# Banded attention with a gated feed-forward block: probabilities turned over by VectorE in 32x32 blocks, values laid per block of 32 keys, and the weighting done in tiles of 32x64 of the array in one visit per group

## The chip, the cores and the metric

The kernel runs on one core of one Trainium2 chip. The metric is the device time of one execution in microseconds (us); a lower time is better. The core has five engines that run at once and wait for each other through semaphores: TensorE (PE in the profile, with its weight loads shown apart as PEld), VectorE (DVE), ScalarE (ACT), GpSimd (POOL) and SyncE (SP), whose queue issues most of the DMAs here.

## The reference: what is computed

Eight batches, eight heads, 576 positions, 64 numbers per head, all float32.

```
scores = q @ k^T / 8                                  # per batch and head, 576 x 576
heads 0-3: keys 0..31 back;   heads 4-7: keys 0, 4, 8, ... 124 back (32 keys each)
attn = softmax(masked scores);   x = attn @ v         # joined over heads: 576 x 512 per batch
h = relu(x @ w_in)            # 512 -> 1024, halves u and v
v_n = (v - mean) / sqrt(var + 1e-6)                   # over the 512 features
v_s = w_spatial @ v_n + b_spatial                     # mixes the 576 positions
out = (u * v_s) @ w_out                               # 512 -> 512
```

So each query looks at 32 keys, its own band. With the positions of heads 4-7 sorted by their residue modulo 4, that band is a plain band too: a block of 32 queries needs the 64 keys of its own block and of the block before.

## The kernel before, in words

**Data.** `NB` = 18 blocks of 32 queries per head. Heads go in pairs (`NPAIR` = 4 per batch): 64 numbers of one head on partitions 0-63, the other's on 64-127. Two pairs make a group (`NG` = 2 per batch), so there are 16 groups in all.

**Scores, `unit` (L417).** A group has `NU` = 3 units; each covers 6 of the 18 blocks, for both pairs and both heads of a pair, by 24 float32 matmuls (L437) with 64 rows and 32 columns of the array. In a score tile the partitions are four sets of 32 queries, and along a row lie `US` = 3 tiles by 2 heads by `KW` = 64 keys: 384 numbers. For the first two batches (`early`) a bfloat16 matmul against the mask stands ahead of each score matmul (L436), and ScalarE takes the exponential straight from PSUM; later batches add the mask on VectorE (L474). Then come the row maximum, the exponential, the row sum, its reciprocal (L484) and the product on GpSimd (L486): the probabilities `p`.

**Turning over.** The weighting needs keys on the partitions. Three TensorE transposes per unit (L491, 128x128, against `ident`) put `p` into a PSUM bank, and ScalarE copies the bank to `pT` (L494): keys of head j on partitions 64j to 64j+63.

**Values, `values_in` (L405).** Each pair has its own buffer: for each block of queries the 64 keys that it needs, head 0 on partitions 0-63 and head 1 on 64-127. Blocks overlap by 32 keys, so each value is loaded twice. Four DMAs per pair, in pieces of 64 numbers.

**Weighting, `weighted` (L500).** Two visits per group, one for each half of the blocks (`HB` = 9). A visit has 36 float32 matmuls (L517), each over 64 keys and giving 64 x 32 numbers, on four tiles of 64 rows by 64 columns of the array. A float32 matmul shows in the trace as two weight loads (PEld) and two multiplications (PE), so a visit is `x72` there. `evacuated` (L533) then splits the result into two parts, `xth` on ScalarE (L543) and `xtl` on VectorE (L256), for the feed-forward block; every large matmul of that block is done in three passes over such parts.

**The rest.** `v_tile` makes the v half (L569, L583), `gate` the u half (L637) and the spatial mix (L648 to L650) with their product (L653), `project` the output (L673, L677, and the store L679). `weight` splits the weights at the start, on ScalarE (L295, L334) and VectorE (L297 to L328) or GpSimd (L312 to L318). `warm` (L689) multiplies zeros at the start.

**What sets the order.** Every piece of work is a generator (a strand) that yields the engine and a cost that it expects, or the buffers that it needs. `Timeline.run` plays these costs through and issues whatever could start first, with a bonus for a lower rank. So the order on each engine is fixed at build time by a table of costs: transposes of a unit 0.45 us on PE and 0.48 us on ACT, a weighting visit 0.9 us. Buffers that are in short supply: 8 PSUM banks, six `kqv` buffers shared by queries with keys and by values, three `p` and four `pT`. At the start the list `first` (L698 to L713) sets the order of the loads.

Of the kernel before, what the change touches and what calls it, by code (L numbers as in the profile page):

```python
# [12 lines left out]
F32 = mybir.dt.float32  # L13
# [108 lines left out]
def tile_banded_attention_gated_moe(  # L122
# [33 lines left out]
    NB = S // QB  # L156
    NS = NB // 2
    US = 3
    NU = NS // US
    NG = NPAIR // 2  # L160
    NC = DM // P
# [5 lines left out]
    EPS = 1e-6  # L167

    BIG = NB * D

    const = ctx.enter_context(tc.tile_pool(name="const", bufs=1))
    work = ctx.enter_context(tc.tile_pool(name="work", bufs=2))
# [2 lines left out]
    def bufs(tag, shape, n, pool=const):  # L175
        return [pool.tile(shape, F32, name=f"{tag}{i}") for i in range(n)]
# [6 lines left out]
            bank=bufs("bank", [P, 512], 8, ps),  # L183
            mm=[None] * 4,
            s=[None] * 2,
            pt=[None] * 2,
            av=[None] * 4,
            wk=[None] * 1,
            kqv=bufs("kqv", [P, WIN + 2 * S], 6),
            stage=[t[:, n * BIG : (n + 1) * BIG] for t in stage for n in range(2)],  # L190
            mid=bufs("mid", [P, 512], 6),
            p=bufs("p", [P, US, 2, KW], 3),
            pT=bufs("pT", [P, US, P], 4),
            ur=bufs("ur", [P, HS], 4),
            ob=bufs("ob", [P, HS], 2),
        )
# [30 lines left out]
            g, row = divmod(c, QB)  # L227
            cut.update({(far, g): 2, (far, g + 1): 3} if row else {(far, g): 1})
    for (far, g), n in cut.items():
        r = slice(g % 2 * 2 * QB, g % 2 * 2 * QB + 2 * QB)  # L230
        nc.vector.tensor_copy(masks[r, US * far + g // 2], kinds[r, n])
    ident = const.tile([P, P], F32, name="ident")
    make_identity(nc, ident)
    same = const.tile([P, P], BF16, name="same")
    nc.vector.tensor_copy(same, ident)
    halfneg = const.tile([P, 1], F32, name="halfneg")
    nc.gpsimd.memset(halfneg, -0.5)

# [143 lines left out]

    used, keys, values = {}, {}, {}

    def heads_in(b, hp, lo=0, hi=NU):

        if lo == 0:
            yield "kqv"
        else:
            yield [("qk", b, hp, lo - 1)]  # L390
        got = yield DMA, 0.83 * (hi - lo), 1.5
        if lo == 0:
            used[b, hp] = got
            keys[b, hp] = got[0][1]
        kq = keys[b, hp]
        w = S // NU
        kc = slice(lo * w + WIN * (lo > 0), hi * w + WIN)
        nc.sync.dma_start(kq[:, kc], kT[b, hp, :, kc])
        nc.sync.dma_start(
            kq[:, WIN + S + lo * w : WIN + S + hi * w].rearrange("p (u c) -> p u c", c=w), qT[b, hp, :, lo:hi]  # L400
        )
        for u in range(lo, hi):
            tl.done("qk", b, hp, u)

    def values_in(b, hp):  # L405

        yield "kqv"
        (big,) = yield DMA, 2.5, 1.5
        src = vw[b, hp].rearrange("k (t j d) -> k t j d", j=2, d=D)
        dst = big[1][:, :BIG].rearrange("p (t n d) -> p t n d", n=2, d=D)  # L410
        for j in range(2):
            for n in range(2):
                nc.sync.dma_start(dst[j * D : j * D + D, :, n, :], src[n * QB : n * QB + KW, :, j, :])
        values[b, hp] = big
        tl.done("values", b, hp)

    def unit(b, G, u):  # L417

        n = (b, G, u)
        pairs = (2 * G, 2 * G + 1)  # L420
        yield [("qk", b, hp, u) for hp in pairs] + ([("v", 0, 1)] if b == 1 else [])
        yield "s bank bank p"
        early = b < 2
        *held, pb = yield PE, 1.1 if early else 0.9
        s = [h[:, : US * KW].rearrange("p (e k) -> p e k", e=US) for _, h in held[1:]]
        for e in range(US):
            for q in range(4):
                g = 2 * (US * u + e) + q // 2
                kq = keys[b, pairs[q % 2]]
                for j in range(2):  # L430
                    r = slice(j * D, j * D + D)
                    if early:

                        kind = cut.get((G >= NG // 2, g), 0)
                        one = same[r, j * D : j * D + QB]
                        nc.tensor.matmul(s[j][q * QB : q * QB + QB, e, :], one, kinds[r, kind], start=True, stop=False)  # L436
                    nc.tensor.matmul(  # L437
                        s[j][q * QB : q * QB + QB, e, :],
                        kq[r, WIN + S :].rearrange("p (u n i t) -> p u t n i", n=2, i=QB, t=US)[:, u, g // 2 % US, g % 2],
                        kq[r, g * QB : g * QB + KW],  # L440
                        start=not early,
                        stop=True,
                    )
# [40 lines left out]
        nc.vector.reciprocal(rv, sm)  # L484
        yield POOL, 0.88
        nc.gpsimd.tensor_mul(flat, flat, rv.unsqueeze(2).broadcast_to([P, 2 * US, KW]))  # L486
        yield "pt bank pT"
        *held, probs[n] = yield PE, 0.45
        pp = held[1][1][:, : US * P].rearrange("k (e q) -> k e q", e=US)
        for e in range(US):  # L490
            nc.tensor.transpose(pp[:, e, :], p[:, e].rearrange("p j k -> p (j k)"), ident)  # L491
        tl.give(pb)
        yield ACT, 0.48
        nc.scalar.copy(probs[n][1], pp)  # L494
        tl.give(*held)
        tl.done("pT", *n)

    probs = {}

    def weighted(b, G, rank):  # L500

        pairs = (2 * G, 2 * G + 1)
        for h in range(2):
            blocks = range(h * HB, h * HB + HB)
            units = sorted({g // 2 // US for g in blocks})
            yield [("pT", b, G, u) for u in units] + [("values", b, hp) for hp in pairs]
            yield "av bank av bank"
            got = yield PE, 0.9
            acc = [got[:2], got[2:]]
            for g in blocks:  # L510
                u, e = divmod(g // 2, US)
                for i, hp in enumerate(pairs):
                    v = values[b, hp][1][:, :BIG].rearrange("p (g d) -> p g d", g=NB)
                    q = g % 2 * 2 + i
                    for j in range(2):
                        r = slice(j * D, j * D + D)
                        nc.tensor.matmul(  # L517
                            acc[j][1][1][i * D : i * D + D, (g - h * HB) * QB : (g - h * HB + 1) * QB],
                            v[r, g, :],
                            probs[b, G, u][1][r, e, q * QB : q * QB + QB],  # L520
                            start=True,
                            stop=True,
                        )
            for u in range(NU):
                if u * US * 2 + US * 2 - 1 in blocks:
                    tl.give(probs[b, G, u])
            if h:
                for hp in pairs:
                    tl.give(values[b, hp])
            for j in range(2):  # L530
                tl.add(rank, evacuated(b, 2 * G + j, h, acc[j]))

    def evacuated(b, hp, h, acc):  # L533
        xh, xl = xt[b % 2]
# [160 lines left out]
    AO, AS = 0.1, 0.6  # L695
    tl.add(0.5, warm())

    first = [heads_in(0, hp, lo, hi) for lo, hi in ((0, 1), (1, NU)) for hp in (0, 1)]  # L698
    halves = {}
    for half in (1, 0):  # L700
        cols = slice(half * NF, half * NF + NF)
        for c in range(NC):

            heads = [c // 2 * 4 + c % 2 + n for n in (0, 2)]
            src = tuple(w_in[h * D : h * D + D, half] for h in heads)
            halves[half, c] = weight_in(("wi", half, c), src)
# [13 lines left out]
    for b in range(B):  # L720
        for hp in range(NPAIR):
            r = b - 1 + AO + AS * hp / NPAIR
            if b:
                tl.add(r, heads_in(b, hp))
                tl.add(r, values_in(b, hp))
# [78 lines left out]
```

## Time and profile before

| | |
|---|---|
| runs of the kernel before | 587.33, 583.3, 587.29 us; median 587.29 |
| the profiled execution | 584.25 us, of which the span from first to last instruction is 582.4 us |
| granted TensorE clock, mean over the span | 0.976 |
| busy in the span: PE, PEld, DVE, ACT, POOL | 547.7, 506.8, 324.1, 242.6, 139.1 us |
| one batch in the steady part (for instance from 394.7 to 459.3 us) | 64.6 us |

How to read it: each engine works through its own instructions in order, so an engine that is late holds up all that is queued behind it. The share of busy time is a mean over stages that have different limits. Here there are two: a start of about 104 us, in which weights are loaded and split while the first batches go through attention, and a long part in which one batch's feed-forward block runs beside the attention of batches ahead. Rows of the timeline give start, duration, engine, line and operation; the durations of TensorE instructions overlap, so a stretch of TensorE work is read from one start to the next.

### The profile page before, as it was taken

The page shows a single profiled execution, that of the slowest core. Times are in us where ns is not written, and L with a number is a line of the kernel's source. Part 1 is how long each engine was busy: PE and PEld are TensorE (multiplying, and loading weights), DVE is VectorE, ACT ScalarE, POOL GpSimd, SP SyncE. Part 2 cuts the span into 40 slices and gives each one's busy share as a digit, 9 for nine tenths or more (in the row PEclk, how much of TensorE's full clock was granted, in tenths as well). Part 3 has the DMA queues.
Part 4 walks back from the last instruction along what each step waited for, and adds up shares of the span by engine and source line. Part 5 has one row for each costly group of instructions (what it writes and reads, how often), then busy time and mean ns, then how long its engine had stood idle before and what let it go on. Part 6 is the DMA issues. An engine that isn't in the chain of part 4 may idle for free.

```text
span 582.4 us, 18304 instructions
## 1 busy us (share of the span) xinstructions
PE 547.7 (94%) x7971; PEld 506.8 (87%) x7971; DVE 324.1 (56%) x775; ACT 242.6 (42%) x620; POOL 139.1 (24%) x163
## 2 busy tenths in 40 slices
PE   9786537999999999999999999999999999999997
PEld 7565537998999989999999989999999989999997
DVE  3799977334863366434863376444863466444411
ACT  3764856433444334333434344343443334423321
POOL 2112987001421023201420033201420132201000
PEclk9979688999999999999999999999999999999999
DMA  8986481631345203731345104731365003101011
GB/s 238 217 218 174 138 215 42 161 93 42 85 119 150 55 12 98 194 83 42 85 130 149 44 12 107 185 84 42 84 156 137 31 19 78 43 1 42 1 42 41
DMA packets 97444, 56.66 MB, mean 97 GB/s; under 512 B 78290, under 2 KB 87506, under 8 KB 97364
## 3 DMA queue, kind: packets, MB, share of 16 engines
q1 hardware_dynamic: 88148, 46.06, 32.2%
q10 hardware_dynamic: 9216, 9.44, 4.6%
q8 instruction: 62, 1.02, 0.7%
q14 instruction: 18, 0.15, 0.1%
HBM read 46.04 MB, written 9.44 MB: 95 GB/s over the span
## 4 chain that ended last, share of the span: by engine, by line
PE 85%; DVE 8%; ACT 2%; DMA 1%; POOL 1%; issue 1%; SPq 1%; ACTq 0%; DVEq 0%; POOLq 0%
PE bank L637 17%; PE bank L648 17%; PE bank L673 17%; PE bank L569 13%; PE bank L517 6%; PE bank L437 5%; PE bank L491 3%; PE bank L689 2%; PE bank L583 2%; PE bank L650 1%; PE bank L649 1%; DVE mid L297 1%; DMA out_dram<-ob 1%; DMA stage<-in_b_sp_dram 1%; DVE bank L299 1%
## 5 line engine op out<-in xcount | busy, mean ns | idle before, releaser
L604 POOL TENSOR_TENSOR rs<-rs,halfneg 128x1 f32<-128x1 f32 (+1 forms) x40 | 31.2, 782 | 245.5 <-DVE rs L602 245.5
L637 PE MATMUL bank<-xth,wih 128*128 128x288 f32 x256 | 79.5, 310 | 0.0
L648 PE MATMUL bank<-wth,vnh 128*128 128x288 f32 x256 | 79.5, 310 | 0.0
L653 DVE TENSOR_TENSOR ur<-ur,bank 128x288 f32<-128x288 f32 x64 | 28.7, 449 | 87.5 <-PE bank L650 87.4
L648 PE MATMUL bank<-wtl,vnh 128*128 128x288 f32 x256 | 76.5, 299 | 0.0
L648 PE MATMUL bank<-wth,vnl 128*128 128x288 f32 x256 | 76.4, 299 | 0.0
L637 PE MATMUL bank<-xth,wil 128*128 128x288 f32 x256 | 75.9, 297 | 0.4 <-issue 0.4
L673 PE MATMUL bank<-gh,woh 128*128 128x288 f32 x256 | 76.2, 298 | 0.0
L637 PE MATMUL bank<-xtl,wih 128*128 128x288 f32 x256 | 76.0, 297 | 0.0
L673 PE MATMUL bank<-gl,woh 128*128 128x288 f32 x256 | 75.7, 296 | 0.1
L673 PE MATMUL bank<-gh,wol 128*128 128x288 f32 x256 | 75.6, 295 | 0.0
L486 POOL TENSOR_TENSOR p<-p,rv 128x384 f32<-128x384 f32 x48 | 40.3, 841 | 80.8 <-DVE rv L484 74.1
L659 ACT CAST gh<-ur 128x288 fp32r<-128x288 f32 x64 | 27.6, 433 | 64.2 <-DVE ur L653 64.2
L569 PE MATMUL bank<-wih,xth 128*128 128x512 f32 x128 | 50.7, 396 | 0.9 <-DVE xtl L256 0.9
L569 PE MATMUL bank<-wil,xth 128*128 128x512 f32 x128 | 50.2, 392 | 0.0
L637 PEld LDWEIGHTS bank<-xth,wih 128*128 128x128 f32 x256 | 48.6, 190 | 1.8 <-ACT p L461 0.2
L569 PE MATMUL bank<-wih,xtl 128*128 128x512 f32 x128 | 50.2, 392 | 0.0
L648 PEld LDWEIGHTS bank<-wth,vnh 128*128 128x128 f32 x256 | 49.0, 191 | 0.8 <-issue 0.2
L437 PEld LDWEIGHTS bank<-kqv 64*32 64x32 f32 x2304 | 32.1, 124 | 20.0 <-issue 19.6
L517 PEld LDWEIGHTS bank<-pT,kqv 64*64 64x64 f32 x2304 | 38.5, 139 | 12.5 <-issue 4.8
L677 ACT COPY ob<-bank 128x288 f32<-128x288 f32 x64 | 25.5, 399 | 57.1 <-PE bank L673 40.5
L648 PEld LDWEIGHTS bank<-wtl,vnh 128*128 128x128 f32 x256 | 49.1, 192 | 0.2
(101 smaller groups left out, 1215.9 us busy)
## 6 DMA issues: line engine op xcount, KB each, us to landing
kqv<-in_vw_dram SPq DMA_DIRECT2D x128, 144.0 KB, 4.1
out_dram<-ob ACTq DMA_DIRECT2D x64, 144.0 KB, 1.7
kqv<-in_kT_dram SPq DMA_DIRECT2D x30, 304.0 KB, 3.3
kqv<-in_qT_dram SPq DMA_DIRECT2D x30, 288.0 KB, 4.3
stage<-in_w_in_dram SPq DMA_DIRECT2D x16, 256.0 KB, 5.3
stage<-in_w_out_dram SPq DMA_DIRECT2D x4, 512.0 KB, 3.5
stage<-in_w_spT_dram SPq DMA_DIRECT2D x5, 288.0 KB, 3.3
kqv<-in_kT_dram SPq DMA_DIRECT2D x2, 192.0 KB, 3.5
```

Source lines behind the costliest of these rows:

```text
L437: nc.tensor.matmul(s[j][q * QB : q * QB + QB, e, :], kq[r, WIN + S :].rearrange("p (u n i t) -> p u t n i", n=2, i=QB, t=US)[:, u, g // 2 ...
L486: nc.gpsimd.tensor_mul(flat, flat, rv.unsqueeze(2).broadcast_to([P, 2 * US, KW]))
L491: nc.tensor.transpose(pp[:, e, :], p[:, e].rearrange("p j k -> p (j k)"), ident)
L517: nc.tensor.matmul(acc[j][1][1][i * D : i * D + D, (g - h * HB) * QB : (g - h * HB + 1) * QB], v[r, g, :], probs[b, G, u][1][r, e, q * QB ...
L569: nc.tensor.matmul(pm, x[a][:, c, cols], wi[w][:, c, NF:], start=c == 0 and n == 0, stop=c == NC - 1 and n == 2)
L604: nc.gpsimd.tensor_tensor(rs[:m], rs[:m], halfneg[:m], op=ALU.pow)
L637: nc.tensor.matmul(pu, wi[w][:, c, fs], x[a][:, c, ts], start=n == 0, stop=n == 3 * NC - 1)
L648: nc.tensor.matmul(pv, vn[c][a][:, fs], wt[w][:, c, ts], start=n == 0, stop=False)
L653: nc.vector.tensor_mul(ur, ur, pv)
L659: nc.scalar.copy(gated[0][:, f, ts], ur)
L673: nc.tensor.matmul(po, wo[w][:, f, ds], gated[a][:, f, ts], start=n == 0, stop=n == 3 * NC - 1)
L677: nc.scalar.copy(ob[1], po)
```

## The change

The probabilities are no longer transposed as a whole. VectorE turns each 32x32 block over where it stands (one instruction of 128x384 per unit, `STREAM_TRANSPOSE`, from one `p` buffer into a second one). Within a set of 32 partitions, keys then lie on the partitions and queries along the row, in four pieces: two heads by two blocks of 32 keys. The transposes on TensorE, their PSUM bank, the copy on ScalarE and `pT` go; there are seven `p` buffers.

So that each of the four sets of 32 partitions has its own values, these are laid per block of 32 keys: set `h * 2 + i` holds half `h` of the blocks of pair `i`, ten blocks with both heads side by side (640 numbers). Each value is loaded once but for the block at the seam. One buffer per group, four DMAs of 32 partitions each, in pieces of 128 numbers. The units' blocks are dealt accordingly: partitions 0-63 take blocks of the first half, 64-127 of the second.

The weighting is one visit per group. Each of the nine tiles has two key blocks by two heads by four sets: 144 float32 matmuls per group with 32 rows and 64 columns of the array and 32 numbers along the row, where there were 72 with 64 rows. The two key blocks are added up in PSUM. Eight tiles of the array are in use instead of four, and four PSUM banks are held at a time, as many as two visits held.

Queries and keys of a pair are loaded by two DMAs from the start, where the first two pairs had them in two parts, and the list `first` is in another order. A part of `w_in` is loaded by one DMA of 128 rows, not by two of 64, since the order of the heads in `x` is now the plain one.

```diff
-            pt=[None] * 2,
-            kqv=bufs("kqv", [P, WIN + 2 * S], 6),
+            kq=bufs("kq", [P, WIN + 2 * S], 4),
+            v=bufs("v", [P, NK, 2 * D], 2),
-            p=bufs("p", [P, US, 2, KW], 3),
-            pT=bufs("pT", [P, US, P], 4),
+            p=bufs("p", [P, US, 2, KW], 7),
...
+    def values_in(b, G):
+        yield "v"
+        (values[b, G],) = yield DMA, 2.6, 1.5
+        v = values[b, G][1]
+        for h in range(2):
+            for i in range(2):
+                src = vw[b, 2 * G + i].rearrange("(r k) (t c) -> k r t c", r=3, c=2 * D)
+                dst = v[(h * 2 + i) * QB : (h * 2 + i + 1) * QB].rearrange("k (r t) c -> k r t c", r=2)
+                nc.sync.dma_start(dst, src[:, h : h + 2, h * (HB // 2) : h * (HB // 2) + NK // 2])
...
-                g = 2 * (US * u + e) + q // 2
+                g = US * u + e + q // 2 * HB
...
         nc.gpsimd.tensor_mul(flat, flat, rv.unsqueeze(2).broadcast_to([P, 2 * US, KW]))
-        yield "pt bank pT"
-        *held, probs[n] = yield PE, 0.45
-        pp = held[1][1][:, : US * P].rearrange("k (e q) -> k e q", e=US)
-        for e in range(US):
-            nc.tensor.transpose(pp[:, e, :], p[:, e].rearrange("p j k -> p (j k)"), ident)
+        yield DVE, 0.52
+        nc.vector.transpose(turned[n][1].rearrange("p e j k -> p (e j k)"), p.rearrange("p e j k -> p (e j k)"))
         tl.give(pb)
-        yield ACT, 0.48
-        nc.scalar.copy(probs[n][1], pp)
-        tl.give(*held)
...
     def weighted(b, G, rank):
+        yield [("turned", b, G, u) for u in range(NU)] + [("values", b, G)]
+        yield "av bank av bank av bank av bank"
+        got = yield PE, 1.8
+        acc = [got[2 * q : 2 * q + 2] for q in range(4)]
+        for t in range(HB):
+            p = turned[b, G, t // US][1]
+            for c in range(2):
+                for j in range(2):
+                    for q in range(4):
+                        r = slice(q * QB, q * QB + QB)
                         nc.tensor.matmul(
-                            acc[j][1][1][i * D : i * D + D, (g - h * HB) * QB : (g - h * HB + 1) * QB],
-                            v[r, g, :],
-                            probs[b, G, u][1][r, e, q * QB : q * QB + QB],
-                            start=True,
-                            stop=True,
+                            acc[q][1][1][j * D : j * D + D, t * QB : t * QB + QB],
+                            values[b, G][1][r, (t + c) % 2 * (NK // 2) + (t + c) // 2, j * D : j * D + D],
+                            p[r, t % US, j, c * QB : c * QB + QB],
+                            start=c == 0,
+                            stop=c == 1,
                         )
...
-    first = [heads_in(0, hp, lo, hi) for lo, hi in ((0, 1), (1, NU)) for hp in (0, 1)]
+    first = [heads_in(0, 0), heads_in(0, 1)]
-    first += [heads_in(0, 2), halves[1, 0], heads_in(0, 3), values_in(0, 0), values_in(0, 1), halves[1, 1]]
-    first += [halves[1, 2], values_in(0, 2), halves[1, 3], values_in(0, 3)] + [halves[0, c] for c in range(NC)]
+    first += [heads_in(0, 2), heads_in(0, 3), halves[1, 0], values_in(0, 0), halves[1, 1], values_in(0, 1)]
+    first += [halves[1, c] for c in (2, 3)] + [halves[0, c] for c in range(NC)]
```

The planner works out a new order from its costs. Three places of it matter for the prediction. In the changed kernel the weighting stands at L497, the turning over at L478, the copies out of PSUM at L518; L436 and L437 become L426 and L427.

On TensorE, in the middle of a weighting. Before, a visit of the first half of a group's blocks: `bank_72` and `bank_68` are the accumulators of the two heads, `kqv_74` and `kqv_75` the values of the two pairs.

```order
L517 MATMUL bank_72<-pT_92,kqv_74 64x32
L517 MATMUL bank_68<-pT_92,kqv_74 64x32
L517 MATMUL bank_72<-pT_92,kqv_75 64x32
L517 MATMUL bank_68<-pT_92,kqv_75 64x32
L517 MATMUL bank_72<-pT_92,kqv_74 64x32
```

Now:

```order
L625 MATMUL bank_70<-wb,vb 128x288
L497 MATMUL bank_73<-p_92,v_78 64x32
L497 MATMUL bank_72<-p_92,v_78 64x32
L497 MATMUL bank_67<-p_92,v_78 64x32
L497 MATMUL bank_69<-p_92,v_78 64x32
L497 MATMUL bank_73<-p_92,v_78 64x32
```

Matmuls that follow each other went to four tiles of the array in turn, and now go to eight: four sets of rows, each with its own bank, and after every four the other half of the columns.

On VectorE, in a batch of the long part, where the probabilities of a unit get ready. Before (`rv` is the reciprocal of the row sums, `ur` and `gl` belong to the gate):

```order
L482 TENSOR_REDUCE sm_0_1_2189<-p_87 128x6
L483 TENSOR_SCALAR sm_0_1_2189<-sm_0_1_2189 128x6
L484 RECIPROCAL rv_0_1_2190<-sm_0_1_2189 128x6
L653 TENSOR_TENSOR ur_93<-ur_93,bank_70 128x288
L256 TENSOR_TENSOR gl<-ur_93,gh 128x288
L482 TENSOR_REDUCE sm_0_2_2253<-p_88 128x6
```

Now:

```order
L474 RECIPROCAL rv_0_1_2420<-sm_0_1_2419 128x6
L628 TENSOR_TENSOR ur_93<-ur_93,bank_68 128x288
L472 TENSOR_REDUCE sm_0_2_2483<-p_89 128x6
L473 TENSOR_SCALAR sm_0_2_2483<-sm_0_2_2483 128x6
L474 RECIPROCAL rv_0_2_2484<-sm_0_2_2483 128x6
L256 TENSOR_TENSOR gl<-ur_93,gh 128x288
L478 STREAM_TRANSPOSE p_91<-p_88 128x384
L628 TENSOR_TENSOR ur_94<-ur_94,bank_67 128x288
L478 STREAM_TRANSPOSE p_86<-p_89 128x384
```

The turning over of units 1 and 2 stands a few instructions behind the reciprocals, among the products of the gate; the last one is behind `ur_94`, which waits for a gate's matmuls on TensorE.

On ScalarE, at the start: the second part of `w_in` to be split (L295) and what stands ahead of it. Before (L543 takes the first weighted result out of PSUM):

```order
L464 ACTIVATE sm_1_0_481<-sm_1_0_481 128x6
L494 COPY pT_91<-bank_70 128x384
L543 CAST xth_155<-bank_67 128x288
L295 ACTIVATE bank_70<-stage_64 128x512
L543 CAST xth_155<-bank_68 128x288
```

Now:

```order
L454 ACTIVATE sm_0_2_388<-sm_0_2_388 128x6
L334 CAST wih<-bank_73 128x512
L295 ACTIVATE bank_71<-stage_64 128x512
L451 ACTIVATE p_92,sm_1_0_459<-bank_68,nm_1_0_458 128x64
```

The second part of `w_in` stood behind the first weighted result; now it follows the third unit's row sums and the first part, and the weighted results (L518) come after the third part.

More of the change, by code (lines that the diff above doesn't have):

```diff
@@ L169, in tile_banded_attention_gated_moe @@
     BIG = NB * D
+    NK = HB + 1
     const = ctx.enter_context(tc.tile_pool(name="const", bufs=1))
@@ L229, in tile_banded_attention_gated_moe @@
     for (far, g), n in cut.items():
[L230 to L233, printed above, removed]
+        r = slice(g // HB * 2 * QB, g // HB * 2 * QB + 2 * QB)
+        nc.vector.tensor_copy(masks[r, US * far + g % HB], kinds[r, n])
     same = const.tile([P, P], BF16, name="same")
-    nc.vector.tensor_copy(same, ident)
+    make_identity(nc, same)
     halfneg = const.tile([P, 1], F32, name="halfneg")
@@ L383, in tile_banded_attention_gated_moe, with heads_in @@
     used, keys, values = {}, {}, {}
[L385 to L415, printed above, removed]
+    def heads_in(b, hp):
+        yield "kq"
+        used[b, hp] = yield DMA, 2.5, 1.5
+        keys[b, hp] = kq = used[b, hp][0][1]
+        nc.sync.dma_start(kq[:, : WIN + S], kT[b, hp])
+        nc.sync.dma_start(kq[:, WIN + S :].rearrange("p (u c) -> p u c", u=NU), qT[b, hp])
+        tl.done("qk", b, hp)
+    def values_in(b, G):
[7 more added lines that the diff above has]
+                nc.sync.dma_start(dst, src[:, h : h + 2, h * (HB // 2) : h * (HB // 2) + NK // 2])
+        tl.done("values", b, G)
     def unit(b, G, u):
@@ L420, in unit @@
         pairs = (2 * G, 2 * G + 1)
-        yield [("qk", b, hp, u) for hp in pairs] + ([("v", 0, 1)] if b == 1 else [])
-        yield "s bank bank p"
+        yield [("qk", b, hp) for hp in pairs] + ([("v", 0, 1)] if b == 1 else [])
+        yield "s bank bank p p"
         early = b < 2
-        *held, pb = yield PE, 1.1 if early else 0.9
+        *held, pb, turned[n] = yield PE, 1.1 if early else 0.9
         s = [h[:, : US * KW].rearrange("p (e k) -> p e k", e=US) for _, h in held[1:]]
@@ L438, in unit @@
                         s[j][q * QB : q * QB + QB, e, :],
-                        kq[r, WIN + S :].rearrange("p (u n i t) -> p u t n i", n=2, i=QB, t=US)[:, u, g // 2 % US, g % 2],
+                        kq[r, WIN + S :].rearrange("p (u n i t) -> p u t n i", n=2, i=QB, t=US)[:, g // 2 // US, g // 2 % US, g % 2],
                         kq[r, g * QB : g * QB + KW],
@@ L486, in unit @@
         nc.gpsimd.tensor_mul(flat, flat, rv.unsqueeze(2).broadcast_to([P, 2 * US, KW]))
-        yield "pt bank pT"
-        *held, probs[n] = yield PE, 0.45
-        pp = held[1][1][:, : US * P].rearrange("k (e q) -> k e q", e=US)
-        for e in range(US):
-            nc.tensor.transpose(pp[:, e, :], p[:, e].rearrange("p j k -> p (j k)"), ident)
-        tl.give(pb)
-        yield ACT, 0.48
-        nc.scalar.copy(probs[n][1], pp)
-        tl.give(*held)
-        tl.done("pT", *n)
-    probs = {}
@@ L500, in weighted @@
-    def weighted(b, G, rank):
[L502 to L517, printed above, removed]
-                            acc[j][1][1][i * D : i * D + D, (g - h * HB) * QB : (g - h * HB + 1) * QB],
-                            v[r, g, :],
-                            probs[b, G, u][1][r, e, q * QB : q * QB + QB],
-                            start=True,
-                            stop=True,
-                        )
[L524 to L531, printed above, removed]
@@ new lines, in unit @@
+        yield DVE, 0.52
+        nc.vector.transpose(turned[n][1].rearrange("p e j k -> p (e j k)"), p.rearrange("p e j k -> p (e j k)"))
+        tl.give(pb)
+        tl.done("turned", *n)
+    turned = {}
+    def weighted(b, G, rank):
+        yield [("turned", b, G, u) for u in range(NU)] + [("values", b, G)]
[8 more added lines that the diff above has]
+                        r = slice(q * QB, q * QB + QB)
+                        nc.tensor.matmul(
+                            acc[q][1][1][j * D : j * D + D, t * QB : t * QB + QB],
[3 more added lines that the diff above has]
+                            stop=c == 1,
+                        )
+        tl.give(*(turned[b, G, u] for u in range(NU)), values[b, G])
+        for q in range(4):
+            tl.add(rank, evacuated(b, 2 * G + q % 2, q // 2, acc[q]))
@@ L702, in tile_banded_attention_gated_moe @@
         for c in range(NC):
-            heads = [c // 2 * 4 + c % 2 + n for n in (0, 2)]
-            src = tuple(w_in[h * D : h * D + D, half] for h in heads)
-            halves[half, c] = weight_in(("wi", half, c), src)
+            halves[half, c] = weight_in(("wi", half, c), (w_in[c * P : c * P + P, half],))
             r = -1.05 if half else -0.5
             tl.add(r + c * 0.05, weight(("wi", half, c), wi[0][:, c, cols], wi[1][:, c, cols], w_in.dtype, half == 0 and c > 1))
-    first += [heads_in(0, 2), halves[1, 0], heads_in(0, 3), values_in(0, 0), values_in(0, 1), halves[1, 1]]
-    first += [halves[1, 2], values_in(0, 2), halves[1, 3], values_in(0, 3)] + [halves[0, c] for c in range(NC)]
+    first += [heads_in(0, 2), heads_in(0, 3), halves[1, 0], values_in(0, 0), halves[1, 1], values_in(0, 1)]
+    first += [halves[1, c] for c in (2, 3)] + [halves[0, c] for c in range(NC)]
     first += [spatial_in(c) for c in (4, 0, 1, 2, 3)]
@@ L724, in tile_banded_attention_gated_moe @@
                 tl.add(r, heads_in(b, hp))
-                tl.add(r, values_in(b, hp))
+                if hp % 2:
+                    tl.add(r, values_in(b, hp // 2))
         for G in range(NG):
```

## The prediction

> **What bounds the kernel now.** I read the page's busy times first, then the sums by stage, then the chain that ended last.
>
> ```profile
> PE 547.7 (94%) x7971; PEld 506.8 (87%) x7971; DVE 324.1 (56%) x775; ACT 242.6 (42%) x620; POOL 139.1 (24%) x163
> ```
>
> ```profile
> core 0: us, PE busy (x) PEld busy (x) DVE busy (x) ACT busy (x) POOL busy (x), PEclk, DMA share, GB/s
> 0.00:14.00 14.00, 12.96 (x253) 10.28 (x253) 4.06 (x20) 4.10 (x16) 3.03 (x14) 1.00 0.88 240
> 14.00:29.00 15.00, 11.12 (x360) 8.88 (x351) 11.30 (x28) 12.03 (x62) 2.48 (x3) 0.98 1.13 218
> ...
> 58.00:73.00 15.00, 8.07 (x108) 7.54 (x107) 14.55 (x34) 11.98 (x41) 13.91 (x14) 0.66 0.49 145
> ...
> 134.00:334.00 200.00, 200.00 (x2903) 187.08 (x2902) 109.61 (x275) 78.78 (x170) 43.07 (x51) 1.00 0.35 94
> 334.00:530.00 196.00, 195.66 (x2871) 183.21 (x2870) 109.90 (x278) 77.08 (x167) 44.80 (x52) 1.00 0.29 74
> ```
>
> ```profile
> PE 85%; DVE 8%; ACT 2%; DMA 1%; POOL 1%; issue 1%; SPq 1%; ACTq 0%; DVEq 0%; POOLq 0%
> ```
>
> From 104 us on TensorE never rests: 200.00 of 200 us and 195.66 of 196 us, at the full granted clock. Whatever TensorE is relieved of there comes off the end, and whatever is added to it goes on. VectorE has 110 of 200 us of work there. Before 104 us it is another kernel: between 58 and 73 us VectorE works 14.55 of 15 us and TensorE 8.07. The chain has 8% VectorE, and it lies in that start. So I cost the change twice: for TensorE from 104 us on, for VectorE before it.
>
> **The change part by part.** First, how much of it lies in the bound part:
>
> ```profile
> L517 PE MATMUL bank<-pT,kqv 64*64 64x32 f32 x1872 | 32.1, 220 | 0.3 <-ACT pT L494 0.3
> L491 PE MATMUL bank<-ident,p 128*128 128x128 f32 x114 | 18.8, 278 | 0.0
> ```
>
> These are the groups from 104 to 530 us. 114 transposes are 38 units; 1872 multiplications at 72 a visit are 26 visits, so 13 of the 16 groups.
>
> *Transposes off TensorE.* Busy time is of no use here, since durations overlap; I read from start to start. Large matmuls of 288 columns start 0.13 us apart.
>
> ```profile
> 289.61 0.30 PE L650 MATMUL bank<-wb,vb 97*128 97x288 f32 x1
> 289.75 0.49 PE L491 MATMUL bank<-ident,p 128*128 128x128 f32 x3
> 290.00 0.38 PE L648 MATMUL bank<-wth,vnh 128*128 128x288 f32 x1
> 290.21 0.30 PE L648 MATMUL bank<-wtl,vnh 128*128 128x288 f32 x1
> ```
>
> From the last large matmul before to the second one after are 0.60 us; two steps of 0.13 us are their own, so three transposes cost 0.34 us. 38 units: **-12.9 us**.
>
> *The weighting.* A visit by itself, and two that the planner had put together:
>
> ```profile
> 184.09 0.29 PE L637 MATMUL bank<-xth,wil 128*128 128x288 f32 x1
> 184.31 1.25 PE L517 MATMUL bank<-pT,kqv 64*64 64x32 f32 x72
> 185.49 0.40 PE L648 MATMUL bank<-wth,vnh 128*128 128x288 f32 x1
> 185.73 0.29 PE L648 MATMUL bank<-wtl,vnh 128*128 128x288 f32 x1
> ```
>
> ```profile
> 441.59 0.30 PE L650 MATMUL bank<-wb,vb 97*128 97x288 f32 x1
> 441.82 2.30 PE L517 MATMUL bank<-pT,kqv 64*64 64x32 f32 x144
> 444.05 0.40 PE L637 MATMUL bank<-xth,wih 128*128 128x288 f32 x1
> 444.29 0.29 PE L637 MATMUL bank<-xtl,wih 128*128 128x288 f32 x1
> ```
>
> In the same way one visit costs 1.38 us and two in one 2.44 us. The second 72 multiplications cost 1.06 us, 14.7 ns each, and 0.32 us of a visit is fixed: the way into the small tiles and out of them. A group before cost 2.44 us (together) to 2.76 us (apart); since visits also stood next to scores and shared the fixed part, I take 2.55 us.
>
> Now a group has 288 multiplications, with a weight load each, on eight tiles. The trace has none of 32 rows; its price lies between these rows:
> - Below: if the four tiles set the 14.7 ns, eight halve it, 288 x 7.35 ns + 0.32 = 2.44 us.
> - Middle: what TensorE's front end delivers. In the early batches the scores go to eight tiles (64x32) already, and each masked score is one small bfloat16 matmul and one float32 matmul. Two single instructions late in such a visit:
>
> ```profile
> 12.19 0.20 PE L436 MATMUL bank<-kinds,same 64*32 64x64 bf16 x1
> ...
> 12.39 0.20 PE L436 MATMUL bank<-kinds,same 64*32 64x64 bf16 x1
> ```
>
>   The second is the mask of the eighth score after the first, 0.20 us on, so 25 ns for three weight loads and three multiplications: 8.3 ns a pair. 288 x 8.3 + 0.32 = 2.7 us; with a pause after the first burst, as in the next row, 2.75 us.
> - Above: two units of scores of a late batch together.
>
> ```profile
> 364.18 0.29 PE L650 MATMUL bank<-wb,vb 97*128 97x288 f32 x1
> 364.40 1.27 PE L437 MATMUL bank<-kqv 64*32 64x64 f32 x96
> 365.60 0.41 PE L637 MATMUL bank<-xth,wih 128*128 128x288 f32 x1
> ```
>
>   From start to the next start 1.20 us for 96 multiplications, 12.5 ns each, though eight tiles were in use: 288 x 12.5 + 0.32 = 3.9 us.
>
> I take 2.75 us, since the changed visit is long, as a steady stream is, and its multiplications (32 columns) are half as long as those of the scores. Against 2.55 us: +0.2 us x 13 = **+2.6 us**, with ends at -0.11 x 13 = -1.4 us and +1.35 x 13 = +17.6 us.
>
> [...]
>
> *ScalarE and VectorE in the bound part.* A unit's copy of 0.49 us (L494 below) leaves ScalarE, and one turning over comes to VectorE. The trace has none; the nearest rows:
>
> ```profile
> L482 DVE TENSOR_REDUCE sm<-p 128x6 f32<-128x384 f32 x36 | 19.8, 549 | 8.0 <-ACT p L480 8.0
> L222 DVE COPY masks<-kinds 128x768 bf16<-128x768 bf16 x1 | 0.4, 360 | 0.0
> L372 DVE CAST wb<-stage 1x576 fp32r<-1x576 f32 x2 | 2.6, 1306 | 1.2 <-DMA stage<-in_b_sp_dram 1.2
> L494 ACT COPY pT<-bank 128x384 f32<-128x384 f32 x48 | 23.0, 487 | 27.8 <-PE bank L491 24.5 <-ACT ob L677 2.1 <-PE bank L650 1.2
> ```
>
> An instruction that reads the same 384 numbers takes 0.55 us, which I take; the bounds are 0.36 us and 384 x 1306 / 576 = 0.87 us. Six units per batch of 64.6 us are 3.3 us on an engine that is idle for some 29 us of it: **0 us**, hidden behind TensorE's feed-forward matmuls. What it costs if that cover is gone is the third rival. The number of evacuations (four per group, L543 and its VectorE part) stays the same.
>
> *DMAs and queues.* Values come in 64 DMAs instead of 128, and less is loaded (each value about once, not twice). In the bound part no wait of TensorE is for values, so **0 us**; SyncE has less to issue.
>
> *The start.* Here VectorE sets the pace, and the chain shows why it began late:
>
> ```profile
> 23.75 0.02 ACT xth L543
> 23.77 0.07 issue
> 23.84 0.02 ACTq L543
> 23.86 0.06 issue
> 23.93 0.02 ACTq L461
> 23.94 0.08 issue
> 24.02 0.68 ACT bank L295
> 24.70 0.02 issue
> 24.73 0.70 DVE mid L297
> ```
>
> The second part of `w_in` could not be split before ScalarE had taken out a weighted result; VectorE was busy for only 4.06 of the first 14 us and 11.30 of the 15 us after them. In the changed order that part (L295) is ahead of all weighted results, and its split can begin up to about 5 us earlier, as VectorE has that much idle time before. In return the six turnings of batch 0 stand among the splits: 6 x 0.55 = 3.3 us. The first scores start later, since 29 zero matmuls instead of 13 stand ahead of them, but two units follow at once. Bounds -5 us and +3.3 us; I take **-2 us**, as the idle time is on the rows and the turnings partly fall into it.
>
> *Sum.* -12.9 + 2.6 - 2 = -12.3 us on the profiled execution of 584.25 us: 572 us. The median of the runs is 587.29 us, 3.0 us above it, so the forecast for the median is **575 us**.
>
> **The rivals.**
> 1. *Eight tiles do not run together as four do* (slower). If four sets of rows cannot be fed or written at once, the 288 multiplications go at the 14.7 ns of the four-tile row: 4.55 us a group, +2.0 x 13 = +26 us, and 575 - 2.6 + 26 = 598 us. It turns to a loss from about 3.7 us a group on, where +1.15 x 13 us eat the 12.9 and the 2 us. For it: no row with 32-row tiles exists. Against: the score visits keep eight tiles at 8.3 ns a pair.
> 2. *The upper row holds*: 3.9 us a group, from pauses such as those that make 12.5 ns out of 8.3 ns in the late scores. 575 - 2.6 + 17.6 = 590 us, no difference that shows. For it: it is the only steady eight-tile row of float32 alone. Against: its pauses come with short visits of 48.
> 3. *The turning over comes late.* The last one of a group is queued on VectorE behind a product of the gate, and the one big visit waits for all three units, where the first of two visits waited for two. If TensorE waits 1 us per group: +13 us, 588 us. Against: from a unit's scores to its last turning lie 2 x 0.35 + 0.55 on VectorE and some 4 us on the others, 5 to 6 us, and the new order puts at least two mixes and two gates (28 and 24 matmuls at 0.13 us, 6.9 us) between.
> 4. *The start gets worse* by 3.3 us rather than better by 2: 580 us, still faster.
>
> **How the numbers follow.** The forecast with the fourth rival has 0.62, and its own range is 567 to 582 us (the ends of the start, the lower end of the weighting). Rival 1 has 0.12, rival 2 0.14, rival 3 0.12. A measurement of this kernel tells apart about 1%, 6 us. Faster by over 1% (below 581.4 us): the forecast's cases but for 0.01, and a third of rivals 2 and 3 (0.05, if they come half), 0.66. Slower by over 1%: rival 1, and 0.02 where rivals add up, 0.14. Within 1%: 0.20. The range of 8 in 10 runs from 566 to 592 us and leaves out most of rival 1 and little below.
>
> **What would show it.** Right: no transposes on TensorE; a weighting of x288 that takes 2.6 to 2.9 us from start to next start; a turning over of about 0.55 us; TensorE busy all through from about 102 us; a batch of some 63 us (64.6 - 6 x 0.34 + 2 x 0.2). Wrong: a weighting over 3.7 us; waits of TensorE for VectorE's turned probabilities of more than some tenths of a us per group; a bound part that begins after 107 us.

## The result, and the profile after

| | before | after |
|---|---|---|
| median of the runs | 586.49 us (583.3 to 587.33) | 635.81 us (633.18 to 636.62) |
| ratio, 95% interval | | 1.084 (1.079 to 1.090) |
| the profiled execution, its span, its mean granted clock | 584.25, 582.4 us, 0.976 | 636.62, 634.8 us, 0.917 |

The change makes the kernel 8.4% slower, and the forecast said 2% faster. First the page of the changed kernel: busy times, shares of the chain that ended last, and the two groups of instructions that it lists first (busy time in us, mean of one in ns, idle time ahead of them and what ended most of it).

```profile
PE 574.6 (91%) x10141; PEld 532.9 (84%) x10141; DVE 344.0 (54%) x822; ACT 220.6 (35%) x572; POOL 139.5 (22%) x163
...
PE 83%; DVE 9%; issue 6%; ACT 1%; DVEq 0%
...
L497 PE MATMUL bank<-p,v 32*64 32x32 f32 x4608 | 60.1, 241 | 41.0 <-issue 36.1
L497 PEld LDWEIGHTS bank<-p,v 32*64 32x64 f32 x4608 | 55.5, 147 | 46.4 <-issue 40.7
```

TensorE is busy for a smaller share than before (91 against 94%), and its idle time stands at the weighting. The profile puts it down to "issue": the engine waited for nothing that the profile shows, no semaphore, no data. The sums by stage, in the windows of the prediction:

```profile
104.00:134.00 30.00, 24.92 (x595) 24.22 (x595) 11.04 (x30) 11.60 (x45) 3.34 (x4) 0.78 0.35 107
134.00:334.00 200.00, 189.65 (x3271) 176.97 (x3270) 107.65 (x274) 63.93 (x138) 41.46 (x48) 0.94 0.20 64
334.00:530.00 196.00, 186.35 (x3222) 174.48 (x3221) 107.26 (x268) 63.38 (x136) 41.42 (x48) 0.96 0.22 68
```

Two things are new in the long part: 10 us without work per window (200.00 of 200 us before), and a granted clock of 0.94 to 0.96 (1.00 before). One visit in the timeline shows the first:

```profile
202.67 0.30 PE L625 MATMUL bank<-wb,vb 97*128 97x288 f32 x1
202.90 2.39 PE L497 MATMUL bank<-p,v 32*64 32x32 f32 x221
207.14 0.88 PE L497 MATMUL bank<-p,v 32*64 32x32 f32 x67 [1.85 <-issue]
207.95 0.40 PE L623 MATMUL bank<-wth,vnh 128*128 128x288 f32 x1
208.18 0.29 PE L623 MATMUL bank<-wtl,vnh 128*128 128x288 f32 x1
```

After 221 of 288 multiplications TensorE stops for 1.85 us and then goes on. All 16 visits do so, once in each from the third on, after 168 to 270 multiplications (a pause of 0.35 us in one of them not counted); from start to next start the pause is 1.7 to 2.9 us, 2.2 on average. By the prediction's own way of reading (start to next start, less two large steps) a weighting costs 5.73 us (median of ten; 5.79 is that of all twelve in the six middle batches), not 2.75.

The second, around another such pause (start to end of the window, its length, then busy times; the clock is the third number from the end):

```profile
236.00:240.40 4.40, 4.40 (x35) 4.31 (x33) 3.16 (x9) 1.62 (x4) 2.80 (x3) 1.00 0.08 33
240.40:243.50 3.10, 2.23 (x201) 2.05 (x199) 1.07 (x3) 0.43 (x1) 0.00 (x0) 1.00 0.02 5
243.50:250.30 6.80, 5.88 (x107) 5.82 (x108) 2.40 (x7) 1.45 (x5) 0.00 (x0) 0.51 0.36 101
250.30:254.00 3.70, 3.70 (x59) 3.54 (x58) 1.49 (x4) 0.72 (x2) 0.00 (x0) 0.99 0.00 0
```

The pause begins at 242.4 us; about 1 us later the granted clock is halved for 6.8 us (0.51 in the row, 1.00 in the two ahead of it). The large matmuls behind the visit run slower: in the stretches with the halved clock they start 0.24 us apart, elsewhere 0.13. Between the first batch's end and the seventh's there are ten such halvings, of 3.4 or 6.8 us, 51 us in all, each beginning 1 to 3.5 us after a pause begins; the kernel before had none there.

Where the 52 us of span went, from the last output matmul of each batch: the first batch ends at 148.9 instead of 139.9 us (+9.0), the next six take 72.2 instead of 65.0 us each (+43.3), the last 49.0 instead of 49.1. In those six batches: 12 weightings at 5.73 for 2.55 us are +38.2; 36 units without transposes are -12.2; what is left is +17.3 us. The halved clock outside the visits has that size: 39 of the 51 us lie there, and large matmuls that start every 0.24 us and not every 0.13 lose an estimated 17 us in 39.

### The profile page after: what moved, and what is told of

It is laid out like the page before. It is cut to its first block, busy times and chain, and to the rows that moved or that the text cites. A ratio compares the mean times of both kernels' runs of the same rounds, so it can differ in the third digit from the quotient of the medians.

```text
span 634.8 us, 22525 instructions
## 1 busy us (share of the span) xinstructions
PE 574.6 (91%) x10141; PEld 532.9 (84%) x10141; DVE 344.0 (54%) x822; ACT 220.6 (35%) x572; POOL 139.5 (22%) x163
## 4 chain that ended last, share of the span: by engine, by line
PE 83%; DVE 9%; issue 6%; ACT 1%; DVEq 0%
PE bank L623 19%; PE bank L612 16%; PE bank L648 16%; PE bank L544 12%; PE bank L497 9%; PE bank L427 4%; PE bank L558 2%; PE bank L664 2%; PE bank L625 2%; PE bank L624 1%; DVE mid L297 1%; DVE xtl L256 1%; DVE mid L581 1%; DVE bank L305 1%; DVE bank L322 1%
## 5 line engine op out<-in xcount | busy, mean ns | idle before, releaser
L497 PE MATMUL bank<-p,v 32*64 32x32 f32 x4608 | 60.1, 241 | 41.0 <-issue 36.1
L497 PEld LDWEIGHTS bank<-p,v 32*64 32x64 f32 x4608 | 55.5, 147 | 46.4 <-issue 40.7
L623 PE MATMUL bank<-wth,vnh 128*128 128x288 f32 x256 | 85.6, 335 | 0.3 <-ACT ur L616 0.3
L623 PE MATMUL bank<-wtl,vnh 128*128 128x288 f32 x256 | 82.8, 324 | 0.0
L256 DVE TENSOR_TENSOR xtl<-bank,xth 128x288 fp32r<-128x288 f32 x64 | 33.6, 569 | 78.9 <-ACT xth L518 78.9
L468 POOL TENSOR_TENSOR p<-p,nm 128x384 f32<-128x384 f32 x36 | 33.9, 942 | 166.7 <-DVE nm L466 166.7
L623 PEld LDWEIGHTS bank<-wth,vnh 128*128 128x128 f32 x256 | 55.2, 215 | 2.2 <-issue 0.5
L623 PEld LDWEIGHTS bank<-wtl,vnh 128*128 128x128 f32 x256 | 55.5, 217 | 0.1
L623 PEld LDWEIGHTS bank<-wth,vnl 128*128 128x128 f32 x256 | 55.1, 215 | 0.0
L518 ACT CAST xth<-bank 128x288 fp32r<-128x288 f32 x64 | 28.6, 572 | 73.6 <-PE bank L497 73.6
```

Source lines behind the costliest of these rows:

```text
L256: nc.vector.tensor_sub(out, a, b.bitcast(F32))
L468: nc.gpsimd.tensor_add(flat, flat, nm.unsqueeze(2).broadcast_to([P, 2 * US, KW]))
L497: nc.tensor.matmul(acc[q][1][1][j * D : j * D + D, t * QB : t * QB + QB], values[b, G][1][r, (t + c) % 2 * (NK // 2) + (t + c) // 2, j * D ...
L518: nc.scalar.copy(dst[0], src)
L623: nc.tensor.matmul(pv, vn[c][a][:, fs], wt[w][:, c, ts], start=n == 0, stop=False)
```

## The experiments

**The theory.** The pause comes from TensorE's supply of instructions. The page's row of the queue that carries instructions, before and then after:

```profile
q8 instruction: 62, 1.02, 0.7%
```

```profile
q8 instruction: 79, 1.29, 0.8%
```

These are packets, megabytes and share: 16 KB a packet. PE and PEld rows together are 15942 before and 20282 after, so 257 records per packet in both. I take a packet to be about 256 instructions, which is 128 pairs of a weight load and a multiplication. Large matmuls use up 128 pairs in an estimated 17 us (0.13 us each), small ones in 1.3 us (9.9 ns from start to start in the first hundred of a visit). If a new piece is asked for only when another is used up, and takes some 3.4 us (no two of these packets start closer together in the changed kernel), a long run of small matmuls outruns it. The rival: the form is to blame, 32 rows, eight tiles, or the number of small matmuls in a row.

**1. The kernel before with as many instructions in a visit.** Its two visits joined, each multiplication issued twice; the tiles stay 64 x 64.

```diff
-        for h in range(2):
-            blocks = range(h * HB, h * HB + HB)
...
+        for g in range(NB):
...
+                for twice in range(2):
                     for j in range(2):
```

> The kernel before, transposes and all, with its two visits joined to one per group and each multiplication issued twice over: 288 per visit, on four tiles of 64 rows. Supply theory: 128 pairs take 1.9 us at 14.7 ns, a piece 3.3 us, so most visits stall for 1 to 1.8 us between pair 128 and 256; 5.5 to 6.5 us a visit, clock below 0.97, 625 to 655 us. Form theory: no stall, 288 x 14.7 ns + 0.3 = 4.55 us a visit, clock as before, about 610 us.

643.44 us, ratio 1.096 (1.089 to 1.102). A visit costs 6.04 us. The rows of one with two pauses:

```profile
463.48 2.52 PE L516 MATMUL bank<-pT,kqv 64*64 64x32 f32 x156
467.13 2.07 PE L516 MATMUL bank<-pT,kqv 64*64 64x32 f32 x128 [1.14 <-issue]
470.87 0.30 PE L516 MATMUL bank<-pT,kqv 64*64 64x32 f32 x4 [1.67 <-issue]
471.10 0.40 PE L631 MATMUL bank<-xth,wih 128*128 128x288 f32 x1
```

The pause is there on the old form and layout, in 13 of the 14 visits from 95 us on, so the form theory falls. It is shorter (mostly 1.0 to 1.8 us for the first of a visit), as the theory would have it: these multiplications take 14.7 ns and cover more of the delivery. There are 128 between two pauses. The clock was halved only twice between 104 us and the end of the work, both times after pauses of 1.9 us.

**2. Same matmuls, half the instructions.**

```diff
-                            values[b, G][1][r, (t + c) % 2 * (NK // 2) + (t + c) // 2, j * D : j * D + D],
-                            p[r, t % US, j, c * QB : c * QB + QB],
+                            values[b, G][1].bitcast(BF16)[r, (t + c) % 2 * (NK // 2) + (t + c) // 2, 2 * j * D + 1 : 2 * j * D + 2 * D : 2],
+                            p.bitcast(BF16)[r, t % US, j, 2 * c * QB + 1 : 2 * c * QB + 2 * QB : 2],
```

> The changed kernel, same order and same 144 matmuls of 32 rows per group in one visit, but each reads only the upper 16 bits of probabilities and values, as bfloat16, so that the lower 16 bits are left out of the weighting and a matmul is one weight load and one multiplication: 144 pairs in place of 288, half the instructions. Supply theory: like the visits of 144 in the run with two visits, a stall only where a piece of 128 pairs ends within the first 16: 0 to 4 stalls in 16 visits, a visit of 1.2 to 1.8 us, 555 to 575 us. If the length of the row of small matmuls or their tiles made the stall, not the instructions, it stays in most visits: over 600 us.

561.58 us, ratio 0.956 (0.951 to 0.961).

```profile
187.00 0.30 PE L625 MATMUL bank<-wb,vb 97*128 97x288 f32 x1
187.23 1.38 PE L497 MATMUL bank<-p,v 32*64 32x32 bf16 x144
188.54 0.41 PE L623 MATMUL bank<-wth,vnh 128*128 128x288 f32 x1
```

With the same 144 matmuls on the same tiles in the same places, 13 of the 14 visits from 97 us on have no pause; one costs 1.51 us. Number, tiles and order of the matmuls are as in the changed kernel, the instructions are half as many. The operands are bfloat16 here, so this run alone does not tell the number of instructions from the type or from the shorter time of a visit; the count under experiment 3 does. (Its time is that of a less precise weighting, so it is no rival to the others as a version.)

**3. Twice the instructions.** The loop over tiles runs twice.

```diff
-        for t in range(HB):
+        for t in (*range(HB), *range(HB)):
```

> The changed kernel with the whole weighting of a group done twice in its visit: 576 pairs in place of 288. Supply theory: once the pieces at hand are used up, each further 128 pairs wait for a piece, so three or four stalls of 1.5 to 2.5 us in a visit, 128 pairs apart, 11 to 14 us a visit, 720 to 780 us. If a visit has one fixed stall, whatever its length: 5.7 + 2.9 = 8.6 us a visit and 670 to 695 us.

787.22 us, one execution. A visit:

```profile
129.35 1.88 PE L497 MATMUL bank<-p,v 32*64 32x32 f32 x170
133.00 1.57 PE L497 MATMUL bank<-p,v 32*64 32x32 f32 x128 [1.76 <-issue]
136.45 2.06 PE L497 MATMUL bank<-p,v 32*64 32x32 f32 x128 [1.89 <-issue]
139.91 2.05 PE L497 MATMUL bank<-p,v 32*64 32x32 f32 x128 [1.39 <-issue]
143.36 0.65 PE L497 MATMUL bank<-p,v 32*64 32x32 f32 x22 [1.40 <-issue]
```

And the DMA queues in the stretch from 129.3 to 143.8 us:

```profile
q8 instruction: 4, 0.07, 1.6%
```

Exactly 128 pairs between pauses, a packet for each of the four. The work goes on 3.5 us after it last went on, and 3.6 us on average over the 37 such stretches from 129 us on (3.45 to 4.0), many at half clock (0.67 on average in the visit above). In the trace's records the next packet mostly starts 1.0 to 1.2 us after the work goes on, up to 0.7 us ahead of the next pause, and takes about 1 us; that pause ends 2.2 to 2.9 us after the packet's start. That a piece is asked for when the one before it is begun is read out of these times; no record shows the asking itself. The time is a little above the expectation, which had not counted that the clock fell to 0.837.

A count settles what the pauses belong to. Number all records of TensorE (matmuls, weight loads and the few of its sequencer) in the order of their start. Then the record behind every stop of 1 us or more (start to next start) after 120 us, up to its last matmul, has the number 193 or 194 modulo 256: 92 of 92 in the traces of all twelve kernels, among them 13 in the changed kernel, 16 in experiment 1 and 48 in this one. Some of the 92 stand in scores, and two of 1.4 and 1.6 us in experiment 2 stand in large matmuls just behind a visit. The kernel before has no such stop in that part. So the stops follow the place in the stream of instructions, in steps of 256, and not the form or the line.

**4. The change's multiplications in two visits, and in three.** The 144 matmuls stay; the planner is made to put about 4 us of other work between.

```diff
+        steps = list(itertools.product(range(HB), range(2), range(2), range(4)))
+        for n, (t, c, j, q) in enumerate(steps):
+            if n == len(steps) // 2:
+                tl.time["gap", b, G] = tl.now + 4.0
+                yield [("gap", b, G)]
+                yield PE, 1.6
```

> The changed kernel with its 288 multiplications per group dealt to two visits of 144, with about 4 us of large matmuls planned between them. Supply theory: TensorE's instructions come in pieces of 16 KB (256 instructions, 128 pairs of weight load and multiplication), a piece is asked for when another is used up, and needs about 3.3 us; 288 pairs in a row run dry, 144 do so only where a piece ends within their first 16 pairs. So 0 to 4 stalls of about 2 us in 32 visits instead of 16 in 16, a visit of 1.6 to 2.0 us, clock 0.96 or more, and a time of 580 to 595 us. Form theory (the stall belongs to matmuls on tiles of 32 rows, however they are dealt): stalls stay in each group, over 620 us.

The three visits have `n in (48, 96)` there and 1.2 us.

> The changed kernel's 288 multiplications per group in three visits of 96, with about 4 us of large matmuls planned between. Supply theory: no stall in the long part, three times 0.96 + 0.35 = 3.9 us a group, so a batch of 64.6 - 2.0 + 2 x (3.9 - 2.55) = 65.3 us and 585 to 597 us. If something else than the supply costs the two-visit run its 617 us, it stays: 605 to 620 us.

617.08 us, 1.051 (1.044 to 1.059), and 605.36 us, 1.030 (1.024 to 1.037). With two visits the pauses in them nearly go: of the 26 halves that stand after 130 us, one lost 1.9 us and three 0.5 or 0.6. A visit of 144 costs 1.79 us, 10.0 ns a multiplication. With three there is none after 130 us. But both times are above what I expected, and the second lies in the range that I had named for a cost other than the supply. One reason is in these rows of the run with two visits, where the planner had put a half between two units of scores:

```profile
313.19 0.75 PE L427 MATMUL bank<-kq 64*32 64x64 f32 x48
313.87 0.84 PE L499 MATMUL bank<-p,v 32*64 32x32 f32 x63
314.98 1.04 PE L499 MATMUL bank<-p,v 32*64 32x32 f32 x81 [0.27 <-issue]
315.95 0.74 PE L427 MATMUL bank<-kq 64*32 64x64 f32 x47
318.98 0.31 PE L427 MATMUL bank<-kq 64*32 64x64 f32 x1 [2.29 <-issue]
```

Between the two pauses lie 81 + 47 = 128 pairs, of two different lines: what counts is the number of instructions, whosever they are. The batch of these rows, with one more such place, took 74.4 us; three of the six took 64.4 to 64.6, as in the kernel before. The first batch costs as much as the six behind it with two visits, and more with three: it ends at 154.4 and 150.3 us (before 139.9). The order that is made for a gap waits in the start, where there is little to put into it. In experiment 7 taking the gap out of the first batch saves 4.0 us; what makes the rest here is not shown. The last batch is longer too (51.7 and 53.6 us for 49.1), which I did not follow up. The six batches between are near what was worked out with three visits, 66.0 us for 65.3, so there the supply theory holds; the whole time does not bear it out.

**5. Fewer matmuls for the same weighting.** A block of values serves the tile that it ends and the tile that it begins; one matmul can read both tiles' probabilities. Within the buffers of a unit that makes 96 matmuls (192 pairs) of 144, in one visit, and in two with the gap of experiment 4.

```diff
-        for t in range(HB):
...
+        for k in (*range(0, NK, 2), *range(1, NK, 2)):
+            tiles = [t for t in (k - 1, k) if 0 <= t < HB]
...
+            w = flat[:, lo : lo + (4 * QB if len(tiles) == 2 else QB)].rearrange("p (n k) -> p n k", k=QB)[:, ::3]
```

> The changed kernel with a block of values held for the two tiles of queries that use it: 96 float32 matmuls of 64 or 32 columns (192 pairs in the trace) in place of 144 of 32 columns (288 pairs), in one visit per group, on the same tiles of 32 rows. Supply theory: a stall only where a piece ends within the first 64 pairs, so in about half of the 16 visits, of 1.5 to 2.2 us; a visit without it 2.3 to 2.8 us; 585 to 605 us. Form theory: a stall in every visit, over 610 us.

> The same 96 matmuls per group in two visits of 96 pairs with about 4 us of large matmuls planned between. Supply theory: no stall, as 96 pairs are less than one piece; a visit of 1.3 to 1.5 us, clock as in the kernel before, 568 to 582 us. Form theory: stalls stay, over 600 us.

In one visit 584.12 us, 0.995 (0.992 to 0.999), a little under the expected range; in two 577.21 us, 0.983 (0.977 to 0.989). Two visits of the kernel with one:

```profile
317.10 1.94 PE L504 MATMUL bank<-p,v 32*64 32x32 f32 x164
321.14 0.45 PE L504 MATMUL bank<-p,v 32*64 32x64 f32 x28 [2.10 <-issue]
...
355.22 2.19 PE L504 MATMUL bank<-p,v 32*64 32x32 f32 x192
```

The same 192 pairs with a pause and without, as the end of a piece falls: of the 13 visits from 120 us on four paused by 1.8 us or more and two by some 0.5. With two visits no visit paused from 99 us on; one costs 1.35 us, and pairs of which half have 64 columns take hardly longer than those of 32 (10.5 and 10.0 ns).

**6. The transposes put back** into the kernel with two visits of 96 pairs.

```diff
+        for e in range(US):
+            nc.tensor.transpose(held[1][1][:, e * P : e * P + P], p[:, e].rearrange("p j k -> p (j k)"), ident)
```

> The merged weighting in two visits (96 matmuls per group) with the three transposes per unit put back on TensorE beside the turning over; what they write is read by nobody. If the prediction's 0.34 us per unit is right, 38 to 42 units in the bound part bring back 13 to 14 us: 588 to 594 us against 577.2. If TensorE had room for them, under 582 us.

592.48 us, 1.011 (1.008 to 1.014): 15.3 us more than without, over 48 units. One of the middle six batches takes 65.5 instead of 63.4 us on average, 0.35 us a unit (three small buffers also went from six to four there, for room). In the profiled executions, which differ by 17.9 us, 5.2 us lie in the first batch.

**7. A version that beats both.** One buffer for the turned probabilities of a group, so that no matmul is cut at a unit's end (80 matmuls), in two visits; then, as the last two lines show against that version, the first batch without the gap.

```diff
+            pt=bufs("pt", [P, HB, 2, KW], 2),
...
-            if n == len(steps) // 2:
+            if b and n == len(steps) // 2:
```

> The merged weighting in two visits once more, with one buffer for the turned probabilities of a group, so that no block of values is cut at a unit's end: 80 matmuls (160 pairs) per group in place of 96, two visits of 80 pairs; for room, five mid and three ur buffers in place of six and four. No stalls in the long part, a visit of about 1.2 us; 0.35 us less per group is some 5 us, so 572 us, 566 to 577; if the fewer buffers cost time, 577 to 590.

> The run with 80 matmuls per group, but with the two groups of the first batch in one visit each (160 pairs), since nothing stands ready there to go between two. If the second visit's place holds up the start, the first batch ends 2 to 4 us earlier than the 142.1 us of that run, and the whole takes 571 to 574 us; if the start is bound by VectorE's splits alone, 574 to 578 us.

575.41 us, 0.980 (0.976 to 0.983), and 571.37 us, 0.973 (0.969 to 0.977). The first batch ends at 142.1 and at 138.1 us. The last one's long part:

```profile
134.00:334.00 200.00, 200.00 (x3061) 185.25 (x3060) 123.16 (x314) 72.39 (x157) 48.17 (x57) 1.00 0.25 79
334.00:530.00 196.00, 195.60 (x2864) 181.65 (x2864) 118.80 (x295) 71.47 (x153) 43.19 (x50) 1.00 0.19 58
```

TensorE is busy throughout again, at the full clock. A batch takes 62.7 us against 65.0; the prediction's way of adding gives 65.0 - 6 x 0.34 + 2 x (2 x 1.22 - 2.55) = 62.7.

## Why the prediction was wrong, step by step

**The step that failed** is the weighting's price, "288 x 8.3 + 0.32 = 2.7 us; ... I take 2.75 us, since the changed visit is long, as a steady stream is". It is the length that was the trouble. All rows behind the price came from runs of 144 pairs at most, and in experiment 3 the pauses stand 128 pairs apart; each visit of the changed kernel had one, after 168 to 270 pairs. Of the 5.73 us, 3.2 are pace (0.35 + 288 x 10.0 ns, from experiment 4; 0.5 more than I took, between my middle and upper row), 2.2 the pause, and the rest, some 0.3, may be its end at the halved clock. So the bounds were bounds of the pace alone, and 3.9 us did not bound the whole; none of the rivals held a wait for instructions, and the slowest of them was 598 us. The halved clock behind the pauses was no term at all: +17 us, a remainder that fits the clock records in size and place but was not tried by itself. In the batches of the long part, pace, pause and halved clock together made +55 us where the prediction had +2.4 for these twelve groups; the first batch, with four paused visits, added 9.0.

The profile before did hold a trace of it. In its chain, in the start:

```profile
21.10 0.94 PE bank L517 x55
22.04 1.20 issue
```

A visit of 72 that stops for 1.20 us after 55, behind other small matmuls, and waits for nothing; by the count of experiment 3 the record behind it has the number 194 modulo 256, as behind the other stops, and the queue's row gives the 128 pairs. I quoted such "issue" rows for ScalarE and passed over this one. Priced at 1.2 us for each of the 13 groups it would have added 16 us: 591 us, no gain.

**Transposes, -12.9 us:** right in size. Experiment 6 gives 0.35 us a unit for 0.34.

**Turning over, 0.55 us, hidden:** right. In the changed kernel:

```profile
L478 DVE STREAM_TRANSPOSE p<-p x48: 536/571/581, 19.8 to 557.5; 128x384 f32<-128x384 f32 x48
...
  PEld bank L497: 0.2, 1
```

That is its line by itself: shortest, median and longest in ns, and who waited for it, in us and times. 0.571 us, and TensorE's loads waited for it once, 0.2 us. The third rival falls.

**The start, -2 us:** the changed kernel's first batch ended 9.0 us later, with two paused visits in the start and two between 100 and 129 us. Where a visit has 144 to 192 pairs and no gap in the start (experiments 2, 5 with one visit, 7 at last), it ends at 137.6 to 138.2 us, 1.7 to 2.3 us earlier than before. That is the size of the forecast. Its reason is not shown: the second part of `w_in` came to ScalarE at 23.04 us in the changed kernel and at 22.10 in the run of experiment 5 with one visit, against 24.02 before, so 1.0 to 1.9 us earlier where up to 5 were allowed, and the first batch also holds a few units without transposes. The fourth rival, a start that is worse for the turnings, does not show in these runs.

**The rivals of the pace.** The turning point (a loss from 3.7 us a group on) agrees: two visits of 1.79 us left undisturbed batches at 64.4 to 64.6 us, about as before, and three that make 3.9 us a group gave 66.0. The first rival's mechanism does not: eight tiles run at 10.0 ns, faster than four at 14.7. The second's 12.5 ns was too slow.

**Short visits and long ones.** In experiment 3, between its pauses, 128 pairs in 3.45 to 4.0 us are 27 to 31 ns a pair, start to start; in visits of 144 a pair takes 10.0 ns (experiment 4). A row of short visits tells nothing of the price in a long one.

## What to carry to other kernels

Count TensorE's instructions, not only its columns. In the long part of these kernels visits of 96 small pairs (experiments 4 and 5) and of 80 (the last of experiment 7) had no pause; of those of 144 (experiment 4) one in 26 lost 1.9 us, of those of 192 four in 13 paused by 1.8 us or more, and those of 288 in the changed kernel paused each, after 168 to 270 pairs. In a visit of 576 the work went on every 3.45 to 4.0 us behind the first pause, for 128 pairs at a time. Before a matmul is split into more and smaller ones, look at the length of the run that this makes and at the "issue" rows; a price read from short runs does not hold for long ones. A pause can cost twice: behind 10 of the 12 in the six batches the granted clock was halved for 3.4 or 6.8 us.

## What the runs showed of the hardware beyond that

- The queue that carries instructions moved 16 KB packets, one per 257 records of PE and PEld (62 before, 79 after), and all 92 long stops stand 256 records or a multiple of that apart in their kernel, give or take one. In the kernel before no stop of 1 us or more shows in that part; in the changed kernel one of 1.7 to 2.9 us stood in each weighting from the third on.
- In the long parts the granted clock is halved (0.50 in its records) for 3.4 or 6.8 us (10.2 to 17.1 us in experiment 3), and that behind most stops of 1.6 us or more: each halving between 104 us and the last microsecond of the work, in all twelve traces, begins within 4.3 us of the start of such a stop, and none behind shorter ones alone.
- On eight tiles of 32 x 64, a float32 pair takes 10.0 ns (experiment 4, 144 in 1.44 us) and a bfloat16 one 8.2 ns (experiment 2, 144 in 1.18 us).
